# Linear attention and a gated feed-forward on one core: means of squares by transposes on VectorE, roots on GpSimd, weight scaling and copies of k^T v on ScalarE

## The chip, the cores and the metric

The kernel runs on one core of one Trainium2 chip. A core has TensorE (matrix products into PSUM), VectorE, ScalarE, GpSimd and a queue engine SyncE that issues most transfers. Each engine works off its own queue in order; semaphores tie the queues together. The time is that of one execution on the device in microseconds, and the median of several runs is compared. In the profile PE is TensorE, PEld its weight loads, DVE VectorE, ACT ScalarE, POOL GpSimd and SP SyncE.

## What is computed

```python
kv  = np.einsum('bhsd,bhse->bhde', k, v)            # 8 batches, 8 heads, 576 rows, 64 columns
o   = np.einsum('bhsd,bhde->bhse', q, kv)
rms = np.sqrt(np.mean(o * o, axis=-1, keepdims=True) + 1e-06)
a   = o / rms * g_norm                               # (8, 8, 576, 64)
x   = a.transpose(0, 2, 1, 3).reshape(4608, 512)
h   = x @ w_in                                       # 512 x 2048
sp  = np.maximum(h, 0) + np.log1p(np.exp(-np.abs(h)))
out = (h * erf(sp)) @ w_out                          # 2048 x 512
```

q, k, v and g_norm are float32. The two weight matrices come as 64-bit floats, which the kernel reads as pairs of 32-bit words.

## The kernel before

**Groups.** The 4608 rows are nine groups of 512: groups 0 to 7 are rows 0 to 511 of each batch, group 8 gathers the 64 rows that each batch leaves over. The attention of a group is worked out in four pairs of heads, called (T, p) with T the group and p the pair. Everything is kept transposed: 128 partitions hold the 2 x 64 columns of a pair, or 128 of the 2048 hidden columns.

**Four stages.** A list written out by hand (`ORDER`) computes the attention of group 0 and prepares the first weights. Then come 16 units of group 0 (n = 0 to 15), one for each 128 hidden columns: a hidden product in plain float32, its copy out of PSUM and the softplus on ScalarE, an Erf, the gate product on VectorE, and five units later (`LAG`) a projection. The attention of group 1 is worked out among them. Then 16 units of group 1 (n = 16 to 31), where the hidden product is made of three parts of lower precision (upper, lower and both), and where the weights are cut into such parts, written to memory and read again later. The attention of group 2 lies among these. The last four units of this stage have no projection between them; `held_sums` makes theirs at the end. From then on (about 240 us) 28 batches of four hidden products and four results follow; in the even ones the attention of the next group is made for two pairs of heads at once (`paired`).

**The order of a unit** (main loop from `for n in range(FIRST * FC + 1)`): perhaps `weights()`; `keep_prepared`; the pieces of place 3; the lower parts of cut weights; the pieces of place 0; `weights()` until what is due is joined; the gate product of unit n - 4 (group 0); the hidden product; its copy and softplus on ScalarE; the pieces of place 1; after every fourth unit of group 0 a batch of four Erf and the reload of the softplus table; the projection of unit n - 5; the pieces of place 2. The order on each engine is the order of the code.

**An attention in group 0's and group 1's units.** `visit` multiplies q by k^T v of its pair (two banks of PSUM, tile `at`), makes the products k^T v of the next pair in the same tile, and squares the result on ScalarE. One unit later `keep_tail` copies the left-over rows and `kv_kept` puts k^T v together: its halves lie in the wrong rows, so VectorE copies them across (line 371) and adds (line 372). `halve` splits the squares in an upper and a lower part, `mean` multiplies both by a matrix of 1/64 on TensorE (lines 470 and 471; for (1, 0) one product in plain float32, line 476), loads the table of logarithms on ScalarE, takes Ln, Exp and Square, and loads the softplus table again unless Erf follows. A unit later `norm` corrects the root by two operations on VectorE (lines 490 and 493), scales o (line 502) and `turn` transposes the next q (line 347). For (1, 0) the products k^T v come by themselves at unit 3 (`prepare`, line 395) and `keep_prepared` at unit 4 copies, adds and turns. The mean of the last pair, (2, 3), is left for `held_sums`.

**Weights.** `weights()` splits one weight tile, joins the one before and loads a later one. A split turns the 64-bit words into numbers: ScalarE scales the lower words (line 271). The upper words are scaled on ScalarE (line 270) during `ORDER`, and afterwards, with `w_late` set, on VectorE at the start of the join (line 281). The join goes on with a shift, an "and/or" and an addition of integers (lines 284, 287, 292).

**A pair of pairs, from 240 us.** `visit`, squares, `keep` (with `two_kept`: four copies on VectorE, line 380, and two adds) at place 2 of a batch; `block_sums` at place 3 (VectorE transposes the squares in blocks of 32x32 and sums 32 columns at a time); `across` at place 4 (four copies of 32x32 on ScalarE bring the sums of the other 32 rows beside them, VectorE adds); `root` at place 5 (Ln, Exp, Square between two table loads); `spread` at place 6 (two corrections, and a transpose of a broadcast that spreads the roots back); `norm` at place 8. Places 1 to 4 follow the four hidden products, 5 to 8 the four results.

**Buffers that matter.** The hidden products of group 1 use two banks by turns within a unit (one for `n_ps`, one for `m_ps`), so each unit needs the copies of the one before. From 240 us three pairs of banks go round. The tile `at` is one buffer.

Of the kernel before, what the change touches and what calls it, by code (L numbers as in the profile page):

```python
# [39 lines left out]
FP32 = mybir.dt.float32  # L40
# [8 lines left out]
EPS = 1e-6  # L49
# [10 lines left out]
BLOCKS = 16  # L60
ORDER = """
# [9 lines left out]
def kernel(  # L71
# [191 lines left out]
    def w_split(which, f, k):  # L263


        hi, lo, _ = words(which, f)
        e = early.tile([P, G * k], I32, name="w_e", tag="w_e", bufs=2)
        m = early.tile([P, G * k], I32, name="w_m", tag="w_m", bufs=2)
        if not w_late:
            nc.scalar.activation(e.bitcast(FP32), hi, AF.Copy, scale=2.0**-112)  # L270
        nc.scalar.activation(m, lo, AF.Copy, scale=2.0**-29)
        w_cv[which, f] = e, m, bool(w_late)

    def w_join(which, f, k):


        scaled, _, hi = words(which, f)
        e, m, late_ = w_cv.pop((which, f))
        w_raw.pop((which, f))
        if late_:  # L280
            nc.vector.tensor_scalar(
                out=e.bitcast(FP32), in0=scaled, scalar1=2.0**-112, scalar2=None, op0=ALU.mult
            )
# [17 lines left out]
    w_late = []  # L301
# [63 lines left out]
    def kv_kept(T, p, at, cols=kv_cols):  # L365
# [4 lines left out]
        for i in range(2):  # L370
            nc.vector.tensor_copy(out=other[rows_of[i]], in_=at[rows_of[1 - i], ::-1, cols])
        nc.vector.tensor_tensor(out=kv, in0=at[:, :, cols], in1=other, op=ALU.add)

    def two_kept(diagonal, beside):
# [3 lines left out]
        for i in range(2):  # L378
            for a, ps in enumerate((diagonal, beside)):
                nc.vector.tensor_copy(out=other[rows_of[i], :, a], in_=ps[rows_of[1 - i]])  # L380
# [22 lines left out]

    def attention(T, p):
# [3 lines left out]
        halves = T > 1 or (T == 1 and p > 0)  # L408
# [4 lines left out]
        two = halves_of  # L413

        bd = kv_of(T, p)

        def square_tile(name):
            return qt_tile(name)[:, 0:G]

        def visit():  # L420
# [24 lines left out]
            nc.scalar.activation(two(st["sq"]), st["o"], AF.Square)  # L445
# [9 lines left out]
        def halve():  # L455
            sq = st.pop("sq")
            hi = st["hi"] = attp.tile([P, G], FP32R, name="sq_hi", tag="rms_r")
            lo = st["lo"] = attp.tile([P, G], FP32R, name="sq_lo", tag="sq_lo")
            nc.vector.tensor_copy(out=hi, in_=sq)
            nc.vector.tensor_tensor(out=lo, in0=sq, in1=hi.bitcast(FP32), op=ALU.subtract)  # L460

        def mean(table=True):
            ms = st["ms"] = st["at"][:, :, 2 * P : 4 * P]
            parts = [(ms[:, a], a) for a in range(2)]
            if halves:


                hi, lo = two(st.pop("hi")), two(st.pop("lo"))
                for ps, a in parts:
                    nc.tensor.matmul(ps, lhsT=mean_w, rhs=hi[:, a], start=True, stop=False)  # L470
                    nc.tensor.matmul(ps, lhsT=mean_w, rhs=lo[:, a], start=False, stop=True)
                u = square_tile("u")
            else:
                u = st.pop("sq")
                for ps, a in parts:
                    nc.tensor.matmul(
                        ps, lhsT=mean_w.bitcast(FP32), rhs=two(u)[:, a], start=True, stop=True
                    )
            r = attp.tile([P, G], FP32, name="rms_r", tag="rms_r")
            exp_ln_table()  # L480
            st["u"], st["r"] = u, r
            nc.scalar.activation(two(r), ms, AF.Ln, bias=eps_col)
            nc.scalar.activation(r, r, AF.Exp, scale=-0.5)
            nc.scalar.activation(u, r, AF.Square)
            if table:
                softplus_table()

        def norm():
            ms, u, r = (st.pop(name) for name in ("ms", "u", "r"))
            nc.vector.scalar_tensor_tensor(  # L490
                out=two(u), in0=ms, scalar=EPS, in1=two(u), op0=ALU.add, op1=ALU.mult
            )
            nc.vector.scalar_tensor_tensor(
                out=u, in0=u, scalar=3.0, in1=r, op0=ALU.subtract, op1=ALU.mult
            )
# [4 lines left out]
            else:  # L500
                x = st["x"] = x_new.tile([P, G], FP32, name="x", tag="x")
            nc.vector.scalar_tensor_tensor(
                out=two(x),
                in0=st.pop("o"),
                scalar=gm_col,
                in1=two(u),
# [29 lines left out]
        pieces = (first_, (visit, loads), (halve, keep_tail) if halves else (keep_tail,))  # L536
        return (*(partial(chain, *group) for group in pieces), mean, partial(chain, norm, then_), split)
# [4 lines left out]
    def paired(T, p):  # L542
# [76 lines left out]
        def small(name):  # L619
            t = twice[name] = attp.tile([P, 2 * BLOCKS], FP32, name=name, tag=name)  # L620
            return t

        def block_sums():


            total = small("ms")
            for n in range(2):
                t = attp.tile([P, G], FP32, name="sq_t", tag=("rms_r", "sq_lo")[n])
                nc.vector.transpose(out=t, in_=twice["x"][n])
                nc.vector.tensor_reduce(  # L630
                    out=total[:, n * BLOCKS : n * BLOCKS + BLOCKS],
                    in_=t.rearrange("p (c d) -> p c d", c=BLOCKS),
                    axis=AX.X,
                    op=ALU.add,
                )

        def across():


# [812 lines left out]
```

## Time and profile before

| | us |
|---|---|
| median of 3 runs | 885.0 (884.7 to 885.28) |
| the profiled execution | 885.01, span 883.2 |
| a mean of squares: L470, L471 MATMUL 128x256, 14 each | 365 and 279 ns each |
| L281 VectorE scaling of upper words x13 | 677 ns |
| L270 ScalarE scaling of upper words, 128x1024 | 1157 ns |
| L371 VectorE copies of halves of k^T v x20 | 288 ns |
| L629, L630, L665 block transpose, sums, spread x24 each | 702, 686, 691 ns |
| L643 ScalarE copies 32x32 x48 | 215 ns |
| L482, L483, L484 Ln, Exp, Square 128x512 | 688, 631, 631 ns |
| table loads L114 x21 and L117 x43 | 1283 ns |

The mean length of a matrix product in the profile is longer than its distance to the next, since they are pipelined: the chain of waits, which counts from start to start, is the view that tells what one costs. The waits of TensorE that the profile puts on another engine are few:

| TensorE or its weight load waits for | us in total |
|---|---|
| VectorE's join of w_in (L292), before hidden products (L1201) | 3.0 |
| VectorE's xT of group 0 (L934) | 1.4 |
| VectorE's held gate parts (L719) | 1.0 |
| the transfer of w_out parts | 0.9 |

The largest waits of all are ScalarE's for TensorE's hidden products (91.8 us before the copy of line 1358) and for VectorE's sums (88.6 us before line 1363): idle time of an engine that isn't the bottleneck.

### The profile page before, as it was taken

What the parts mean: (1) busy time and instruction counts of PE and PEld (TensorE: products, weight loads), DVE (VectorE), ACT (ScalarE), POOL (GpSimd) and SP (SyncE); (2) the same over time, 40 slices, a digit from 0 to 9 for tenths busy, and PEclk for the clock granted to TensorE, in tenths of its full rate; (3) what the DMA queues carried; (4) which work ended last, traced back from release to release, by engine and by line L of the source; (5) the groups of instructions that cost most, each with busy time, mean ns of one, the idle gap of its engine ahead of it and who ended that gap; (6) DMA issues with size and microseconds to landing.
All of it is one profiled execution on the core that took longest, in us unless ns stands there. A gap on an engine that the chain in (4) does not pass through costs nothing.

```text
span 883.2 us, 13286 instructions
## 1 busy us (share of the span) xinstructions
PE 875.1 (99%) x4874; PEld 659.1 (75%) x4874; DVE 752.6 (85%) x1107; ACT 559.3 (63%) x789; POOL 4.7 (1%) x14
## 2 busy tenths in 40 slices
PE   8999999999999999999999999999999999999998
PEld 4444456666788888888888888888888888888887
DVE  5889978899998898989898989898979797966667
ACT  5977677777775657565665647474757575755552
POOL 2000000000000000000000000000000000000000
PEclk9999999999999999999999999999999999999999
DMA  9977427989799997999799979998797779778871
GB/s 291 291 225 224 132 75 285 342 310 341 262 358 401 330 347 251 385 328 349 232 382 350 353 231 346 366 342 295 272 351 282 288 288 344 289 279 334 316 255 49
DMA packets 136929, 259.89 MB, mean 294 GB/s; under 512 B 78816, under 2 KB 87264, under 8 KB 136864
## 3 DMA queue, kind: packets, MB, share of 16 engines
q1 hardware_dynamic: 136128, 258.09, 82.8%
q10 hardware_dynamic: 544, 0.82, 0.3%
q8 instruction: 39, 0.64, 0.3%
q14 instruction: 26, 0.21, 0.1%
q0 software_dynamic: 192, 0.13, 0.0%
HBM read 224.40 MB, written 34.60 MB: 293 GB/s over the span
## 4 chain that ended last, share of the span: by engine, by line
PE 91%; DMA 3%; DVE 2%; ACT 2%; issue 1%; SPq 0%; DVEq 0%; ACTq 0%
PE n_ps L778 48%; PE m_ps L778 24%; PE o_ps L834 8%; PE h_ps L1201 5%; DMA w_out_parts<-w_out 1%; PE at_ps L557 1%; DMA q_sb<-in_q_dram 1%; PE off_ps L588 1%; DMA w_in<-w_new 1%; PE warm_ps L982 1%; DMA w_in_parts<-w_in 0%; PE at_ps L427 0%; ACT s_sb L1154 0%; PE at_ps L440 0%; ACT L1154 0%
## 5 line engine op out<-in xcount | busy, mean ns | idle before, releaser
L778 PE MATMUL n_ps<-w_out_parts,g_forms 128*128 128x512 f32 (+1 forms) x936 | 230.1, 388 | 0.2 <-DMA w_out_parts<-w_out 0.2
L778 PE MATMUL n_ps<-x_forms,w_in_parts 128*128 128x512 f32 x896 | 222.6, 390 | 0.0
L778 PEld LDWEIGHTS n_ps<-w_out_parts,g_forms 128*128 128x128 f32 x936 | 175.0, 188 | 36.7 <-DMA w_out_parts<-w_out 0.9
L778 PEld LDWEIGHTS n_ps<-x_forms,w_in_parts 128*128 128x128 f32 x896 | 167.4, 188 | 35.1
L753 DVE TENSOR_TENSOR h<-m_ps,h 128x512 f32<-128x512 f32 x116 | 78.5, 686 | 58.6 <-PE m_ps L778 58.5
L1358 ACT ACTIVATE h<-n_ps 128x512 f32<-128x512 f32 x112 | 66.7, 596 | 94.0 <-PE n_ps L778 91.8
L1363 ACT ACTIVATE s<-h 128x512 f32<-128x512 f32 x112 | 69.2, 632 | 88.6 <-DVE h L753 88.6
L778 PE MATMUL m_ps<-w_out_parts,g_forms 128*128 128x512 f32 x464 | 123.9, 389 | 0.0
L778 PE MATMUL m_ps<-x_forms,w_in_parts 128*128 128x512 f32 x448 | 119.7, 389 | 0.0
L778 PEld LDWEIGHTS m_ps<-w_out_parts,g_forms 128*128 128x128 f32 x464 | 87.1, 188 | 18.1
L778 PEld LDWEIGHTS m_ps<-x_forms,w_in_parts 128*128 128x128 f32 x448 | 84.1, 188 | 17.5
L753 DVE TENSOR_TENSOR e<-m_ps,e 128x512 f32<-128x512 f32 x116 | 80.1, 692 | 14.1 <-PE m_ps L778 3.4
L834 PE MATMUL o_ps<-w_out_sb,h_sb 128*128 128x512 f32 x192 | 86.8, 595 | 0.0
L713 ACT ACTIVATE g_forms<-h 128x1024 fp32r<-128x1024 f32 x58 | 60.8, 1061 | 39.2 <-PE m_ps L778 21.0
L719 DVE SCALAR_TENSOR_TENSOR g_forms<-g_forms 128x1024 fp32r<-128x1024 f32 x58 | 71.1, 1226 | 2.0
L716 DVE TENSOR_TENSOR g_forms<-h,g_forms 128x1024 fp32r<-128x1024 f32 x58 | 70.5, 1215 | 0.5 <-ACT g_forms L713 0.4
L1412 DVE TENSOR_TENSOR h<-h,s 128x1024 f32<-128x1024 f32 x56 | 65.9, 1217 | 0.0
L834 PEld LDWEIGHTS o_ps<-w_out_sb,h_sb 128*128 128x128 f32 x192 | 35.5, 190 | 38.3 <-issue 36.9
L748 DVE SCALAR_TENSOR_TENSOR e<-n_ps,e 128x512 f32<-128x512 f32 (+1 forms) x89 | 59.8, 671 | 3.4 <-PE n_ps L778 3.4
L1201 PE MATMUL h_ps<-xT,w_in_sb 128*128 128x512 f32 x128 | 57.9, 596 | 1.3 <-DVE w_in_sb L292 1.2
L117 ACT ACT_TABLE_LOAD x43 | 55.2, 1283 | 0.8
L1386 ACT ACTIVATE s<-s 128x1024 f32<-128x1024 f32 x50 | 50.6, 1054 | 0.3
(166 smaller groups left out, 936.6 us busy)
## 6 DMA issues: line engine op xcount, KB each, us to landing
w_out_parts<-w_out SPq DMA_DIRECT2D x116, 768.0 KB, 7.2
w_in_parts<-w_in SPq DMA_DIRECT2D x112, 768.0 KB, 6.7
w_in<-w_new SPq DMA_DIRECT2D x16, 768.0 KB, 4.8
k_sb<-in_k_dram SPq DMA_DIRECT2D x32, 288.0 KB, 6.1
v_sb<-in_v_dram SPq DMA_DIRECT2D x31, 288.0 KB, 5.7
w_raw<-in_moe_w_in_dram SPq DMA_DIRECT2D x16, 512.0 KB, 6.3
w_raw<-in_moe_w_out_dram SPq DMA_DIRECT2D x8, 1024.0 KB, 5.3
out_dram<-e SPq DMA_DIRECT2D x32, 256.0 KB, 4.0
```

Source lines behind the costliest of these rows:

```text
L117: nc.scalar.preload_act_table_set("softplus")
L713: nc.scalar.activation(high, x, AF.Copy, scale=1.0 + 2.0**-13)
L716: nc.vector.tensor_tensor(out=low, in0=x, in1=high.bitcast(FP32), op=ALU.subtract)
L719: nc.vector.scalar_tensor_tensor(out=both, in0=low.bitcast(FP32), scalar=SHIFT, in1=high.bitcast(FP32), op0=ALU.mult, op1=ALU.add,)
L748: nc.vector.scalar_tensor_tensor(out=out_, in0=ps, scalar=scale, in1=out_, op0=ALU.mult, op1=ALU.add)
L753: nc.vector.tensor_tensor(out=out_, in0=ps, in1=out_, op=ALU.add)
L778: nc.tensor.matmul(ps[:, cols], lhsT=weights(form, k), rhs=moving(form, k)[:, cols], start=(form == forms[0] and k == 0), stop=(form == fo ...
L834: nc.tensor.matmul(o_ps[j], lhsT=g[:, j * P : j * P + P], rhs=one(w_out_sb, f), start=(f == 0), stop=last,)
L1201: nc.tensor.matmul(plain[i], lhsT=blocks_of(one(w_in_sb, i % FC))[:, c], rhs=xT[T][:, c, :], start=(c == 0), stop=(c == KC - 1),)
L1358: nc.scalar.activation(h[:, i], n_ps, AF.Copy, scale=SHIFT - 1.0)
L1363: nc.scalar.activation(s[:, i], h[:, i], AF.Softplus)
L1412: nc.vector.tensor_tensor(out=part(h, half), in0=part(h, half), in1=part(s, half), op=ALU.mult)
```

## The change

Every mean of squares is now made as the paired stage made its own: transposes and sums on VectorE, four copies across on ScalarE. The roots are no longer taken from ScalarE's tables but on GpSimd, by a first guess from the number's bits and three Newton steps: 15 operations on 128x16 (or 128x32) that follow one another. The spread by transposes replaces the corrections. ScalarE scales the upper words of all weights, and copies the halves of k^T v in `kv_kept` and `two_kept`. The mean of the last pair is no longer left for the end. The softplus table is loaded after every Erf batch of the paired stage. Gone are the products with the matrix of 1/64 among the units, and the table loads around the roots. The first attention (`ORDER`) is as before.

```diff
+NEWTON = 3
...
-        if not w_late:
-            nc.scalar.activation(e.bitcast(FP32), hi, AF.Copy, scale=2.0**-112)
+        nc.scalar.activation(e.bitcast(FP32), hi, AF.Copy, scale=2.0**-112)
         nc.scalar.activation(m, lo, AF.Copy, scale=2.0**-29)
...
-        if late_:
-            nc.vector.tensor_scalar(
-                out=e.bitcast(FP32), in0=scaled, scalar1=2.0**-112, scalar2=None, op0=ALU.mult
-            )
...
         for i in range(2):
-            nc.vector.tensor_copy(out=other[rows_of[i]], in_=at[rows_of[1 - i], ::-1, cols])
+            nc.scalar.copy(other[rows_of[i]], at[rows_of[1 - i], ::-1, cols])
         nc.vector.tensor_tensor(out=kv, in0=at[:, :, cols], in1=other, op=ALU.add)
...
-                nc.vector.tensor_copy(out=other[rows_of[i], :, a], in_=ps[rows_of[1 - i]])
+                nc.scalar.copy(other[rows_of[i], :, a], ps[rows_of[1 - i]])
...
+    def sums_of_blocks(squares):
+        total = small("ms", len(squares))
+        for n, x in enumerate(squares):
+            t = attp.tile([P, G], FP32, name="sq_t", tag=("rms_r", "sq_lo")[n])
+            nc.vector.transpose(out=t, in_=x)
+            nc.vector.tensor_reduce(
+                out=total[:, n * BLOCKS : n * BLOCKS + BLOCKS],
+                in_=t.rearrange("p (c d) -> p c d", c=BLOCKS),
+                axis=AX.X,
+                op=ALU.add,
+            )
+        return total
+
+    def roots(total):
+        n = total.shape[1] // BLOCKS
+        other, m, y, a = (small(name, n) for name in ("ms_other", "ms_eps", "rms", "rms_a"))
+        for k in range(4):
+            rows, beside = (slice(32 * i, 32 * i + 32) for i in (k, k ^ 1))
+            nc.scalar.copy(other[rows], total[beside])
+        two, one_ = nc.gpsimd.tensor_tensor, nc.gpsimd.tensor_scalar
+        two(out=m, in0=total, in1=other, op=ALU.add)
+        one_(out=m, in0=m, scalar1=EPS, scalar2=None, op0=ALU.add)
+        one_(
+            out=y.bitcast(I32),
+            in0=m.bitcast(I32),
+            scalar1=-0.5,
+            scalar2=float(0x5F3759DF),
+            op0=ALU.mult,
+            op1=ALU.add,
+        )
+        for _ in range(NEWTON):
+            two(out=a, in0=y, in1=y, op=ALU.mult)
+            two(out=a, in0=a, in1=m, op=ALU.mult)
+            one_(out=a, in0=a, scalar1=-0.5, scalar2=1.5, op0=ALU.mult, op1=ALU.add)
+            two(out=y, in0=y, in1=a, op=ALU.mult)
+        return y
+
+    def spread_over(xs, y):
+        for n, x in enumerate(xs):
+            nc.vector.transpose(
+                out=x.rearrange("p (c d) -> p c d", c=BLOCKS),
+                in_=y[:, n * BLOCKS : n * BLOCKS + BLOCKS].unsqueeze(2).to_broadcast([P, BLOCKS, 32]),
+            )
...
-            nc.scalar.activation(two(st["sq"]), st["o"], AF.Square)
+            nc.scalar.activation(halves_of(st["sq"]), st["o"], AF.Square, scale=0.125)
...
+        def block_sums():
+            st["ms"] = sums_of_blocks([st["sq"]])
+
+        def root():
+            st["r"] = roots(st["ms"])
...
-        pieces = (first_, (visit, loads), (halve, keep_tail) if halves else (keep_tail,))
-        return (*(partial(chain, *group) for group in pieces), mean, partial(chain, norm, then_), split)
+        pieces = (first_, (visit, loads), (keep_tail, block_sums), (root,), (norm, then_), (split,))
+        return (partial(chain, *group) for group in pieces)
...
-            pieces = first | {3: (block_sums,), 4: (across,), 5: (root,), 6: (spread,), 8: norms}
+            pieces = first | {3: (block_sums,), 4: (root,), 6: (spread,), 8: norms}
...
-    w_late.append(True)
...
-            steps[f + 2][3].append(halve)
-            with_erf = (f + 2) % BATCH == BATCH - 1
-
-            place = 2 if T < FIRST and p == 0 else 1
+            steps[f + 2][3].append(keep)
+            steps[f + 2][0].append(root)
             if T == FIRST and p == NP - 1:
-                ending.extend((partial(mean, table=False), norm, split))
+                ending.extend((norm, split))
                 continue
-            steps[f + 2][place].append(partial(mean, table=not with_erf))
...
-        mean, norm, split = ending
-        mean()
+        norm, split = ending
...
-            if not last_ and (b % 2 or not todo):
+            if not last_:
                 softplus_table()
```

In `norm` of both kinds the two corrections are replaced by `spread_over`, and o is scaled by `g_col` in place of `gm_col` (which held -0.5 times it).

## The prediction

> **What bounds the kernel now.** I read first the busy shares and the slices of the page.
>
> ```profile
> PE 875.1 (99%) x4874; PEld 659.1 (75%) x4874; DVE 752.6 (85%) x1107; ACT 559.3 (63%) x789; POOL 4.7 (1%) x14
> ...
> DVE  5889978899998898989898989898979797966667
> ```
>
> TensorE never rests for long, so the time is its work plus its few waits; VectorE is nearly full in the first 240 us (slices 2 to 11, of 22 us each), which is where most of the change lies. GpSimd does nothing after its start-up. Then the chain of waits in order of time. Between two products of group 0 stands one mean of squares:
>
> ```profile
> 66.16 3.43 PE h_ps L1201 x8
> 69.59 0.12 PE at_ps L470
> 69.71 0.12 PE at_ps L471
> 69.82 0.12 PE at_ps L470
> 69.94 0.12 PE at_ps L471
> 70.06 3.43 PE o_ps L834 x8
> ```
>
> The reader is to see that a mean costs the bounding engine 70.06 - 69.59 = 0.47 us, and that TensorE runs without a gap on both sides. From 50.78 to 195 us this chain is TensorE alone. Last I read the timeline of the engines at the places where the order of the queues changes (below).
>
> **What the change removes from TensorE.** Eight means: seven at 0.47 us are 3.3 us. The eighth, of (1, 0), is plain float32: TensorE ends a projection at 49.26 and starts the next hidden product at 50.78, 1.5 us with 0.5 us of waiting for weights. So at most 4.8 us, and nothing new is put on TensorE. Were this all, the time would be 885.0 - 4.8 = 880.2. That has to be set against who is now waited for.
>
> **Work that changes engine, by stage.** Group 0's units (22 to 129 us): VectorE loses 13 scalings (677 ns, 8.8 us); per attention it loses the halving (423 + 692), two root corrections (2 x 690) and two copies (2 x 288), and gains a transpose, a reduction and a spreading transpose (702 + 686 + 691): 1.0 us less each. ScalarE gains 13 scalings, 1.16 us by its one row of 128x1024, starting 1.05 apart, and per attention two copies 64x128 and four 32x32 (215 ns). The first are not shown on ScalarE; bounds are its 32x32 copy (215) and its 128x512 copy (586); I take 0.29, VectorE's own for that shape and on the line between the two by columns. ScalarE loses two table loads (1283 each) and three passes (688 + 631 + 631), 4.5 us each. In sums every engine but GpSimd gets lighter. All these hide behind TensorE if order lets them; order doesn't, at two places.
>
> **Place 1: the kv copies stand behind an Erf batch.** Unit 4 begins with `keep_prepared`: two copies of a half of k^T v, an add, and the transpose of q that the visit of (1, 0) multiplies. Unit 3 ended on ScalarE with a table load, four Erf and a table load.
>
> ```profile
> 36.86 0.59 ACT L1214 COPY h_sb<-h_ps 128x512 f32<-128x512 f32 x1 [0.57 <-PE h_ps L1201]
> 37.48 0.63 ACT L1230 ACTIVATE s_sb<-h_sb 128x512 f32<-128x512 f32 x1
> 38.12 1.28 ACT L1154 ACT_TABLE_LOAD   x1
> 39.42 2.19 ACT L1154 ACTIVATE s_sb<-s_sb 128x512 f32<-128x512 f32 x4
> 41.63 1.28 ACT L117 ACT_TABLE_LOAD   x1
> ...
> 37.67 0.59 DVE L371 COPY kv_other<-at_ps 64x128 f32<-64x128 f32 x2 [2.52 <-PE at_ps L395]
> 38.29 0.29 DVE L372 TENSOR_TENSOR bd_kv<-at_ps,kv_other 128x128 f32<-128x128 f32 x1
> 38.57 0.78 DVE L347 STREAM_TRANSPOSE qT<-q_sb 128x576 f32<-128x576 f32 x1
> ...
> 41.11 0.66 PE L427 MATMUL at_ps<-qT,bd_kv 64*64 64x256 f32 x8
> ```
>
> Now VectorE copies at 37.67 while ScalarE is busy, and q is ready at 39.35, before TensorE asks at 41.11. After the change the copies queue behind the Erf batch. ScalarE's new scaling in unit 2 (34.00) delays its chain by 1.05, of which 0.57 is eaten by the wait before 36.86: the last table load ends near 43.3. Two copies end at 43.85, the add at 44.2, the transpose at 45.0. TensorE's visit starts there: **3.9 us late**. Behind the waiting add on VectorE stand the join of w_out 0 (L284, L287, L292: 44.9 to 48.2), gate 0 (to 48.8), the tail copy and add (49.3), the new block sums (50.6) and the join of w_in 6 (3.2 us by its rows, to 53.8). TensorE, from 45.0: visit 1.17, hidden product 3.54, projection 3.43, is free at 53.15 and waits 0.65 for that join. The product that started at 50.78 starts at 53.8: **+3.0 us** with the first mean already taken off. The next units have room: the same ordering strikes at unit 8 (copies behind the Erf of unit 7, VectorE idle some 5 us), but gate 5, which I get at 85.9, is needed at 87.5.
>
> **Between.** Three means of group 0 and three of group 1 (0.47 each) take off 2.8: at unit 29 TensorE is +0.2. There keeps fall in units without Erf, and ScalarE's copies land where it idled (3.7 us before 140.94, 4.8 before 167.78).
>
> **Place 2: the last attention of group 1's stage (unit 30).** Here no projection separates hidden products 30 and 31, and both use the same two banks. On record now:
>
> ```profile
> 218.53 0.60 ACT L1216 ACTIVATE h<-n_ps 128x512 f32<-128x512 f32 x1 [0.37 <-PE n_ps L778]
> ...
> 219.25 0.42 PE L778 MATMUL n_ps<-x_high,w_new 128*128 128x512 f32 x1
> ```
>
> The bank is copied out by 219.13 and product 31 starts. After the change ScalarE's queue between Square (217.3) and that copy holds: two upper halves (to 218.3), four kv copies (to 219.35), then the four copies of `roots`, which wait for VectorE's block sums (adds at 219.7, sums to 221.0): to 221.95. Only then comes the bank's copy, to 222.55, so product 31 starts at 222.6 instead of 219.25. VectorE's `hold_lower` follows the late add (to 225.2 and 226.5), so the second held product starts at 226.55 instead of 224.23. The mean of 0.47 and two short waits that stood there are gone in this: **+2.3 us** from here on. Norm, split and the last gates move by the same 2.2 (the norm no longer waits 1.37 for ScalarE's roots, but VectorE comes later), so the transfers of w_out that start behind the last gates stay as hidden as now.
>
> **The paired stage (from 240 us).** Its TensorE work is the same, VectorE loses 0.55 us of small operations per pair, ScalarE a table load. Its copies of k^T v end when VectorE's did (Squares end 289.4, four copies to 290.4, adds to 291.0; now 291.2). New is that VectorE's spread (304.28 in the batch I followed) waits for 15 dependent GpSimd operations that can start when the 32x32 copies end (297.96). The nearest GpSimd rows are its memset of 128x256 (0.31) and
>
> ```profile
> 9.75 0.22 POOL L232 TENSOR_SCALAR gm_col<-g_col 128x1 f32<-128x1 f32 x1 [4.65 <-DMA g_col<-in_g_norm_dram]
> ```
>
> Between 0.22 and 0.31 us each, 15 make 3.3 to 4.7 us; 5.7 are there. I take 0.3. The next bank is needed at 308.46 and read out by 306.19, so the spread may be 2.3 us late before TensorE waits: GpSimd has 8.5 us in all, 0.57 per operation. Cost taken: nothing. The upper bound is that GpSimd and VectorE only take turns, which no row of this trace can exclude, as GpSimd is idle beside VectorE. In the pairs 2.8 us of VectorE's time before the spread reads one operand from PSUM; if only the two-operand rows (L719, L1412) shut GpSimd out, an operation may cost 0.42. In groups 0 and 1 VectorE has hardly other rows: some six GpSimd operations get in before the spread, the other nine cost 2.7 us and those six delay VectorE by 1.5, 4.2 us per attention. Gate 5 then comes at 90.1, 2.6 us too late for TensorE, and the held products 1 to 2 us later: +4 in sum, 891. A gain below nothing from GpSimd's part is excluded: no engine waits for less by it than is counted above.
>
> [...]
>
> **Sum.** 885.0 - 4.8 (means and the wait beside the first) + 3.9 + 0.65 (place 1) + 2.6 (place 2: 3.35 - 0.2 of late bank, less 0.55 of waits that go) = 887.35, that is 887.3 by the walk. The profiled execution took 885.01 (span 883.2 and 1.8 around it), the median is 885.0, so nothing is to be converted.
>
> **Rivals.**
> - *The gain survives* (881, 0.13): both delays are absorbed. For it: all engines get lighter in sums, and VectorE's 12 us of relief in group 0 might bring joins forward. Against: the visit depends on the late copies directly, and TensorE has no other wait after 50.78 to absorb 3 us. With one of the places absorbed: 884 to 885 (0.09).
> - *GpSimd shares VectorE's time* (891, range 889 to 896, 0.22): above; it decides as soon as spread waits show on VectorE over 3 us.
> - *GpSimd's chain outlasts the pairs' slack* (0.06): at 0.5 us an operation with VectorE shutting it out, the spread comes 3.4 us late, TensorE waits 1.1 us in each of 12 pairs: 887.3 + 4 + 13 = 904. It decides from 0.42 us per operation.
> - That the change doesn't do what it says I exclude: queue order is that of the code, and the rows of now follow it at every place read.
>
> **How the numbers follow.** The forecast (887.3, own range 885.5 to 889) has 0.50. A measurement of this kernel tells 0.2% (1.8 us) from no change: the border to slower is 886.8. Of the forecast 0.16 lies under it, and 0.09 for one place absorbed: same 0.25. Faster 0.13; slower 0.34 + 0.22 + 0.06 = 0.62. The range 883.0 to 893.5 leaves out most of the surviving gain below and the long GpSimd chain and the top of the shared case above.
>
> **What would show it.** Right: a TensorE wait of 3 to 4 us before L427 near 41 to 45 us, with kv copies on ScalarE behind the first Erf batch; a wait of about 3 us before hidden product 31; no means in the chain; steady pairs of 45.9 us for two batches as now. Wrong: the visit still near 41; VectorE waiting for GpSimd at the spreads; two batches longer than 45.9 (the chain's 335.29 to 381.22).

## The result and the profile after

| | before | after |
|---|---|---|
| median of the runs, us | 885.02 (884.7 to 885.28) | 896.21 (895.64 to 897.02) |
| profiled execution, its span, us | 885.01, 883.2 | 897.02, 895.2 |

The ratio is 1.0127 (95% interval 1.011 to 1.0145): slower by 11.2 us, where 2.3 were forecast and 893.5 was the upper end of the range. First the busy shares of the page after:

```profile
PE 879.0 (98%) x4842; PEld 658.7 (74%) x4842; DVE 720.9 (81%) x996; ACT 532.0 (59%) x804; POOL 131.7 (15%) x314
...
PEclk9989999999999999999999999999999999999999
```

TensorE has 32 instructions less and yet 3.9 us more of busy time; VectorE and ScalarE are lighter by 32 and 27 us. The clock that TensorE was granted (PEclk, in tenths of full speed) has a dent in the third of the 40 slices, 45 to 67 us. Next, from the list of waits by engine, TensorE's largest (in total, times, longest):

```profile
PE at_ps L469 <- DVE qT L342: 3.8, 1, 3.8
PE n_ps L746 <- ACT h L1179: 3.4, 1, 3.4
PE o_ps L802 <- DVE h_sb L1046: 2.1, 2, 1.5
```

The first is place 1, the second place 2, the third the gates of group 0. The timeline shows place 1 (start, length, engine, line, operation; in brackets the idle time before and who ended it):

```profile
44.12 0.29 DVE L367 TENSOR_TENSOR bd_kv<-at_ps,kv_other 128x128 f32<-128x128 f32 x1 [8.67 <-ACT kv_other L366]
44.40 0.78 DVE L342 STREAM_TRANSPOSE qT<-q_sb 128x576 f32<-128x576 f32 x1
45.33 1.13 PE L469 MATMUL at_ps<-qT,bd_kv 64*64 64x256 f32 x8 [3.82 <-DVE qT L342]
...
47.45 5.50 PE L1164 MATMUL h_ps<-xT,w_in_sb 128*128 128x512 f32 x8
```

VectorE stands 8.67 us for the copies that ScalarE makes behind its Erf batch, and the visit comes at 45.33 instead of 41.11. That was forecast. The last line was not: a hidden product that took 3.70 now takes 5.50. Place 2 is hidden product 31, whose bank is free only when ScalarE has copied product 30 out of it:

```profile
225.98 0.84 ACT L424 COPY ms_other<-ms 32x16 f32<-32x16 f32 x4 [1.75 <-DVE ms L409]
226.84 0.60 ACT L1179 ACTIVATE h<-n_ps 128x512 f32<-128x512 f32 x1
...
227.49 0.50 PE L746 MATMUL n_ps<-x_high,w_new 128*128 128x512 f32 x1 [3.39 <-ACT h L1179]
227.83 0.40 PE L746 MATMUL n_ps<-x_low,w_new 128*128 128x512 f32 x1
228.06 0.40 PE L746 MATMUL n_ps<-x_high,w_new 128*128 128x512 f32 x1
...
228.53 0.56 PE L746 MATMUL n_ps<-x_high,w_new 128*128 128x512 f32 x1
228.89 0.63 PE L746 MATMUL n_ps<-x_low,w_new 128*128 128x512 f32 x1
229.32 0.63 PE L746 MATMUL n_ps<-x_high,w_new 128*128 128x512 f32 x1
```

The bank's copy stands behind the four copies of `roots`, as forecast, and 1 us later the products go from 0.40 to 0.63 us each; from the start of one to the start of the next they go from 0.23 us (227.83 to 228.06) to 0.43 us (228.89 to 229.32). Compared at four marks (the first two by the chain of waits, the third by the timeline), the loss arises so:

| mark | before | after | late by | new here |
|---|---|---|---|---|
| hidden product 6 | 50.78 | 56.39 | 5.6 | 5.6 |
| first product of group 1 | 128.67 | 134.99 | 6.3 | 0.7 |
| first product of group 2 | 234.90 | 243.38 | 8.5 | 2.2 |
| end of the span | 883.2 | 895.2 | 12.0 | 3.5 |

### The profile page after: what moved, and what is told of

Same layout as the page of the kernel before. It is cut to its first block, busy times and chain, and to the rows that moved or that the text cites. A ratio compares the mean times of both kernels' runs of the same rounds, so it can differ in the third digit from the quotient of the medians.

```text
span 895.2 us, 13467 instructions
## 1 busy us (share of the span) xinstructions
PE 879.0 (98%) x4842; PEld 658.7 (74%) x4842; DVE 720.9 (81%) x996; ACT 532.0 (59%) x804; POOL 131.7 (15%) x314
## 4 chain that ended last, share of the span: by engine, by line
PE 88%; ACT 4%; DVE 3%; DMA 2%; POOL 2%; issue 1%; SPq 0%; DVEq 0%; ACTq 0%
PE n_ps L746 50%; PE m_ps L746 25%; PE o_ps L802 6%; PE h_ps L1164 1%; PE at_ps L567 1%; PE off_ps L598 1%; DMA v_sb<-in_v_dram 1%; DMA w_raw<-in_moe_w_in_dram 1%; PE n_ps L1062 1%; PE warm_ps L950 1%; ACT w_e L270 1%; ACT w_m L271 1%; PE at_ps L469 0%; ACT s_sb L1117 0%; PE at_ps L482 0%
## 5 line engine op out<-in xcount | busy, mean ns | idle before, releaser
L746 PE MATMUL n_ps<-x_forms,w_in_parts 128*128 128x512 f32 x896 | 224.9, 393 | 0.0
L426 POOL TENSOR_TENSOR ms_eps<-ms,ms_other 128x32 f32<-128x32 f32 (+1 forms) x20 | 15.2, 758 | 610.1 <-ACT ms_other L424 610.1
```

The costliest lines, as they stand in the source:

```text
L746: nc.tensor.matmul(ps[:, cols], lhsT=weights(form, k), rhs=moving(form, k)[:, cols], start=(form == forms[0] and k == 0), stop=(form == fo ...
```

## The experiments

Four theories were set against each other: **waits** (the two places), **clock** (TensorE is slower for a while after a rest), **GpSimd** (its chain costs VectorE time, by taking turns or by being waited for) and **layout** (the new small tile shifts all later ones). "Before" and "after" name the two kernels. All medians below stand against 884.9 to 885.1 for the kernel before on the same chip. In several expectations "3.70 us at 91.33" is called TensorE's wait for gate 5; that was a misread column: 3.70 is the length of the products there, the wait is 1.50 us.

### Layout

```diff
-        other, m, y, a = (small(name, n) for name in ("ms_other", "ms_eps", "rms", "rms_a"))
+        other, y, a = (small(name, n) for name in ("ms_other", "rms", "rms_a"))
+        m = other
```

> The sum with epsilon is written over ms_other instead of into a tile of its own, so that one small tile (128 bytes of each partition) is not allocated and all later tiles of that side lie where they lay in the kernel before; instructions and order are the same. Layout theory: the hidden products of the odd groups from 3 on take 2.72 instead of 2.79 us again, 12 batches of four of them, so 3.4 us less: 892.5 to 893.2. Rival (the odd groups' products are slowed by what GpSimd or ScalarE newly do beside them): 896 to 896.5, and 2.79 as before.

892.15 us (ratio to before 1.0078, 1.0061 to 1.0095), 4.1 less than after. And the other way round, in the kernel before:

```diff
-    const.tile([P, 8], FP32, name="pad")
+    const.tile([P, 40], FP32, name="pad")
```

> The kernel before, with an unused tile of constants longer by 128 bytes of each partition, so that all tiles of one side lie 128 bytes further on; not one instruction is different. Layout theory (the odd groups' hidden products depend on where their weights lie against x_forms): 12 batches of four products at 2.79 instead of 2.72 us, 888.0 to 888.6. Rival (the layout only mattered together with what the change does): 884.7 to 885.3.

889.06 us (1.0048, 1.0031 to 1.0064): 4.0 more, with no instruction changed. The groups of TensorE's rows from 240 to 880 us (count, busy time, mean ns of one), of before, after, the run with one tile less and before shifted:

```profile
L778 PE MATMUL n_ps<-x_forms,w_in_parts 128*128 128x512 f32 x880 | 218.7, 390 | 0.0
```

```profile
L746 PE MATMUL n_ps<-x_forms,w_in_parts 128*128 128x512 f32 x896 | 224.9, 393 | 0.0
```

```profile
L747 PE MATMUL n_ps<-x_forms,w_in_parts 128*128 128x512 f32 x896 | 222.7, 390 | 0.0
```

```profile
L778 PE MATMUL n_ps<-x_forms,w_in_parts 128*128 128x512 f32 x880 | 220.9, 393 | 0.0
```

The mean of 393 ns follows the 128 bytes and not the change. It hides two kinds, which the chain of after tells apart (start, length of eight products), an even and an odd group:

```profile
259.58 1.81 PE n_ps L746 x8
```

```profile
346.26 1.87 PE n_ps L746 x8
348.13 0.93 PE m_ps L746 x4
```

Only groups 3, 5 and 7 are slow: 2.79 instead of 2.72 us for a hidden product, 48 of them, 3.4 us. From the first product of group 2 to the end the kernels with the old addresses take 648.3 (before) and 647.7 (one tile less), those with shifted ones 651.8 (after) and 652.5 (before shifted). All 18 profiles fall into these two sets: 647.6 to 648.3 us in the eight kernels with the old addresses, 651.7 to 652.9 us in the ten with shifted ones, whatever else was changed. So the size of the loss at the fourth mark is shown, and its cause is where the tiles lie. Why these addresses are slower the runs do not tell.

### Place 1

```diff
-        kept.append(partial(kv_kept, T, p, at))
+        kept.append(partial(kv_kept, T, p, at, copy=nc.vector.tensor_copy))
```

> The two copies of k^T v that keep_prepared makes for the visit of (1, 0) go back to VectorE; all other copies stay on ScalarE. Waiting theory (the copies stand behind the first Erf batch, and the 4 us of rest cost TensorE's clock another 2 us): the visit starts near 41.2 instead of 45.33 us, hidden product 5 takes 3.54 instead of 5.43 us, and the first hidden product of group 1 comes at 129 to 130.5 instead of 134.99; 890.5 to 892 us in all. Rival (VectorE is short of time in group 0 anyway, so what is won there is lost again at gate 5, for which TensorE waits 3.70 us at 91.33): that wait grows to 6 us or more, and the time stays over 893.5.

895.39 us: 0.8 less than after. Neither theory had it: the time is over 893.5, as the rival said, but the wait for gate 5 did not grow to 6 us, it stayed at 1.48. The visit was on time, at 41.27; the chain tells what came instead:

```profile
43.41 1.14 ACT w_e L270
...
46.61 0.59 ACT qT L487
...
48.05 0.29 DVE bd_kv L367
48.34 0.63 DVE sq_t L408
...
49.59 0.69 DVE w_e L280
50.31 1.24 DVE w_e L283
51.57 1.24 DVE w_in_sb L288
...
52.95 5.37 PE h_ps L1164 x8
```

The new scaling on ScalarE makes the Square late (46.61, before 45.12), then come the copies on ScalarE and the block sums, and behind them the join that hidden product 6 needs, which before started at 46.79. So product 6 waits 3.37 us and again is slow. Two delays stood one behind the other, and taking away the first laid the second bare. To test this, the sums and the root of (1, 0) were put behind that join as well:

```diff
+        keep, root_ = [keep_tail, block_sums], [root]
+        if (T, p) == (1, 0):
+            root_.insert(0, keep.pop())
...
+            steps[f + 2][1 if (T, p) == (1, 0) else 0].append(root)
```

> The changed kernel with the copies for the visit of (1, 0) on VectorE, and with the block sums and the root of (1, 0) issued behind the join that hidden product 6 needs. Join theory (the first experiment won only 0.8 us because the join of w_in 6 then stood last, behind the scaling on ScalarE, the copies and the sums): visit at 41.3, join ended near 51.6, hidden product 6 at 51.6 instead of 52.95 after a wait of 2 us, and not slow; of the 3.4 us that this wins over the first experiment (1.4 of wait, 1.9 of clock) gate 5 may take up to 2 back: 892 to 894. Rival (VectorE's work up to gate 5 is the same, and all of it sets the end): 894.5 to 896.

893.32 us, as the join theory had it: product 6 at 51.33 after a wait of 2.2 us, at full speed (3.67 us), group 1 at 131.02.

### The clock

The first test put eight extra products ahead of the late visit, in a part of its own bank:

```diff
+            for _ in range(8 if (T, p) == (1, 0) else 0):
+                nc.tensor.matmul(prepared[0][:, 0, 0 : 2 * P], lhsT=xT[0][:, 0, 0:P], rhs=xT[0][:, 0, 0 : 2 * P], start=True, stop=True)
```

> The changed kernel with eight extra products in plain float32 (256 columns, into a part of the bank that nobody reads) ahead of the visit of (1, 0), so that TensorE works in the 3.8 us in which it waits for the late copies; the visit still waits. Clock theory (the rest itself makes TensorE slow for some 3 to 4 us afterwards): the visit stays at 45.3, its products and hidden product 5 run at full speed (1.2 and 3.5 us instead of 2.2 and 5.43), hidden product 6 starts at 54.4 when its join ends instead of 56.39. How much of the 2 us reaches the end depends on gate 5: if VectorE's work sets it, the wait at 91.33 grows and the time is 895.3 to 896.3; if not, 894 to 894.6. Rival (hidden product 5 is slow because something disturbs it, not because TensorE rested): 5.4 us as before.

899.17 us, and it did not test what it should: the extra products waited for the late add as well, so TensorE rested 2.97 us all the same, and they themselves took 5.38 us. The slow time fell on them, and hidden product 5 behind them took 3.70. With a free bank they needn't wait:

```diff
+                busy = ps_h.tile([P, G], FP32, name="busy_ps", tag="h")
+                for _ in range(8):
+                    nc.tensor.matmul(busy[:, 0 : 2 * P], lhsT=xT[0][:, 0, 0:P], rhs=xT[0][:, 0, 0 : 2 * P], start=True, stop=True)
```

> The test of the rest again, with the eight extra products in a bank that is free (their result isn't read), so that they needn't wait for the late add. Clock theory: they run from 41.3 to 45, the visit starts at 45.3 to 45.4 at full speed (1.2 us), hidden product 5 starts at 46.8 and takes 3.4 to 3.7 us instead of 5.43, hidden product 6 starts when its join ends, at 54.4, instead of 56.39; gate 5 then sets group 0, so the time is 895.2 to 896.4. Rival: 5.4 us for hidden product 5 as before.

895.37 us, within the clock theory's range. The same eight products took 3.62 us, and hidden product 5 behind the visit 3.70, not 5.50:

```profile
40.65 3.62 PE L469 MATMUL busy_ps<-xT 128*128 128x256 f32 x16
44.64 0.66 PE L479 MATMUL at_ps<-qT,bd_kv 64*64 64x256 f32 x8 [0.37 <-DVE qT L342]
...
45.82 3.70 PE L1174 MATMUL h_ps<-xT,w_in_sb 128*128 128x512 f32 x8
```

It is these lengths that decide; that the time lies in the range is in part luck. The expectation had gate 5 take the gain back. It took nothing: TensorE's wait for it is 1.48 us, as in after, and from the visit to group 1 it is 88.0 us (44.64 to 132.61) instead of 89.7 (45.33 to 134.99). But from group 2 on the profiled execution took 652.9 us instead of 651.8, for which the runs show no reason. The windows from 40 to 50 us (busy TensorE, weight loads, VectorE, ScalarE, GpSimd, then the granted clock, DMA share and GB/s), of after and of this run:

```profile
40.00:50.00 10.00, 6.18 (x55) 3.30 (x54) 5.21 (x9) 8.46 (x15) 0.00 (x0) 0.71 0.58 190
```

```profile
40.00:50.00 10.00, 9.63 (x76) 6.12 (x75) 5.85 (x10) 7.71 (x14) 0.00 (x0) 1.00 0.53 170
```

So this rest of 3.82 us cost twice, by its length and by the clock behind it: 0.71 against 1.00 in these windows. By single microseconds the clock of after is 0.64 in 44 to 45 us, 0.50 from 45 to 51, 0.95 in 51 to 52 and 1.00 from 52 to 55: some six microseconds at half, more than the 3 to 4 that the first expectation here took, an estimate of the author's. Place 2 shows that this has chance in it. The same wait of 3.4 us stands there in after and in this run:

```profile
226.00:230.00 4.00, 2.51 (x8) 2.04 (x9) 2.49 (x4) 3.06 (x8) 2.60 (x7) 0.83 1.08 372
230.00:234.00 4.00, 4.00 (x14) 3.16 (x14) 3.21 (x6) 1.67 (x3) 3.35 (x9) 0.75 0.86 227
```

```profile
224.00:228.00 4.00, 2.93 (x13) 2.40 (x14) 2.91 (x5) 3.14 (x7) 2.94 (x8) 1.00 1.06 355
```

From start to start the eight products behind that wait took 1.96 us here, 2.68 in after, 3.43 in the run with the join first and 3.58 in the run with only the norm later. What the clock cost in after is read against this run, where it stayed at 1.00: from the start of product 31 to the first held product 4.39 us (227.49 to 231.88) against 2.89, to group 2's first product 15.89 against 14.68. So the slow products took 1.5 us more, of which 1.2 reached group 2. The clock of after is 0.80 in 228 to 229 us, 0.50 from 229 to 232 and 0.99 in 232 to 233. Over all profiles the products behind waits of 1.45 to 2.2 us were at full speed (3.67 to 3.70 us for eight of group 0's 128x512, 0.66 for eight of a visit), and behind 18 of the 19 waits of 2.97 us or more they were not, at once or within about 1 us; the nineteenth is the 3.39 us of this run. The shortest with slow products behind them are 2.97 (the first test: 5.38 us for the extra products, which take 3.62 behind no rest) and 3.08 us (the run under "Scaling": 5.11 for eight). Why the same wait was followed by slow products in one run and not in another is not shown.

### Place 2

```diff
-            steps[f + 2][0].append(root)
+            steps[f + 2][1 if T == FIRST and p == NP - 1 else 0].append(root)
```

> The root of the last pair of group 1's units (the four 32x32 copies on ScalarE and the GpSimd chain) is issued one place later, behind the hidden product of unit 31 and its bank's copy; nothing else moves. Waiting theory: the wait of 3.39 us at 227.49 shrinks to about 0.7 (the four k^T v copies stay ahead of the bank's copy), the slow products behind it (2.88 and 1.71 us for halves that take 1.83 and 0.93) are fast again, and the time is 891.5 to 893.3. Rival (the late root only moves the wait to the norm and the held products of the last pair, which need the spread): TensorE waits as long some 10 us later, 895 to 896.5.

894.06 us, 2.2 less than after; 2.9 to 4.7 were expected. The wait is 0.79 instead of 3.39, the products behind it are at full speed (1.97 us from start to start for eight), and group 2 starts at 240.57, 2.8 earlier. Some 0.6 us come back as two waits of the held products for `hold_lower` (0.50 and 0.15). The rival, by which the wait only moves, is wrong by most of the amount.

### GpSimd and VectorE

Does GpSimd's work slow VectorE down? In the kernel before, 15 operations that nobody reads followed each of twelve gates:

```diff
             gates(done)
+            y = attp.tile([P, 2 * BLOCKS], FP32, name="rms_u", tag="rms_u")[:, 0:BLOCKS]
+            x = hs[done][:, 0:BLOCKS]
+            for _ in range(5):
+                nc.gpsimd.tensor_scalar(out=y, in0=x, scalar1=-0.5, scalar2=1.5, op0=ALU.mult, op1=ALU.add)
+                x = y
+                for _ in range(2):
+                    nc.gpsimd.tensor_tensor(out=y, in0=y, in1=y, op=ALU.add)
```

> The kernel before with a chain of 15 GpSimd operations on 128x16 after each of the gates 0 to 11 of group 0, whose result nobody reads: 180 operations in some 78 us, four times what the change puts there, and nothing waits for them. Turns theory (GpSimd and VectorE take turns, and both lose): VectorE's rows with two operands grow or start later, 0.2 us for most operations, some 20 us of VectorE in a stage where it is 94% busy: 890 to 905. Rival (only GpSimd loses: its operations stretch to 1.2 us, VectorE's rows stay, and the change lost time because VectorE waits in its queue for the end of the chain): 884.7 to 886.5, with GpSimd operations of 0.22 to 1.3 us.

885.55 us (1.0006, 0.9997 to 1.0016): no difference. The window of group 0, before and in this run:

```profile
50.00:128.00 78.00, 77.50 (x325) 35.95 (x324) 72.34 (x98) 55.63 (x72) 0.00 (x0) 1.00 0.58 174
```

```profile
50.00:128.00 78.00, 77.50 (x326) 36.14 (x325) 72.50 (x98) 54.88 (x71) 68.02 (x121) 1.00 0.55 174
```

GpSimd was busy for 68 of 78 us beside a VectorE that was busy for 72, and VectorE did its 98 instructions in the same time. Only GpSimd loses. How much is seen in the changed kernel's timeline, beside two-operand rows of VectorE and without them:

```profile
79.90 1.23 DVE L283 SCALAR_TENSOR_TENSOR w_e<-w_raw,w_e 128x1024 int32<-128x1024 int32 x1
80.02 1.19 POOL L438 TENSOR_TENSOR rms_a<-rms_a,ms_eps 128x16 f32<-128x16 f32 x1
...
81.27 1.23 DVE L288 CUSTOM_DVE_ANT_0 w_in_sb<-w_e,w_m 128x2048 uint16<-128x2048 uint16 x1
81.30 1.26 POOL L439 TENSOR_SCALAR rms_a<-rms_a 128x16 f32<-128x16 f32 x1
...
82.64 0.22 POOL L440 TENSOR_TENSOR rms<-rms,rms_a 128x16 f32<-128x16 f32 x1
82.94 0.22 POOL L437 TENSOR_TENSOR rms_a<-rms 128x16 f32<-128x16 f32 x1
...
85.29 0.71 DVE L447 STREAM_TRANSPOSE qT<-rms 128x512 f32<-128x512 f32 x1 [2.79 <-POOL rms L440]
```

While VectorE stands the operations of lines 438 and 439 take 0.22 and 0.20 us (83.24 and 83.55). Beside VectorE's long rows they took 1.19 and 1.26 and ended within 0.08 us of these: at 81.21 and 82.56, the rows at 81.13 and 82.50. Beside the shift of line 280, which has one operand (79.18, 0.69 us), one took 0.53. The chain takes 8.7 us, from 76.55 to 85.25, its second half undisturbed because VectorE stands and waits 2.79 us for it. Behind that wait in VectorE's queue are the spread, the norm, a turn, a join and gate 5 (90.59), for which TensorE waits 1.50 us. That VectorE is held up in its turn shows nowhere here: its 98 instructions took 72.50 us beside GpSimd's work and 72.34 without.

Would the chain be better on VectorE?

```diff
-        two, one_ = nc.gpsimd.tensor_tensor, nc.gpsimd.tensor_scalar
+        engine = nc.vector if n == 1 else nc.gpsimd
+        two, one_ = engine.tensor_tensor, engine.tensor_scalar
```

> The 15 root operations of the seven attentions in groups 0 and 1's units run on VectorE, 128x16 each; those of the pairs stay on GpSimd. Exclusion theory (GpSimd waits while VectorE reads two operands, and VectorE then waits for the chain: 14.5 us before its spreads of the units): VectorE's waits before these spreads go and 15 operations of some 0.07 to 0.15 us take their place, TensorE's wait of 3.70 us for gate 5 at 91.33 shrinks below 2, and the time is 893 to 895. Rival (gate 5 is late because VectorE started its joins late at place 1 and has too much to do): the wait stays 3 us or more, 895.8 to 897.

907.41 us, worse than either theory allowed: 15 operations cost VectorE 3.1 us (0.17 to 0.18 each and 0.21 from start to start, not 0.07 to 0.15, an estimate that no row shows: additions of 128x32 took 0.18 in the kernel before), and all stand ahead of a join. In the first of them the join of product 6 ended at 58.4 and group 1 started at 142.71; the wait at place 2 grew from 3.39 to 4.69.

With only the spread and the norm of the units moved behind the hidden product, and nothing else:

```diff
-            steps[f + 3][0].append(norm)
+            steps[f + 3][0].append(then_turn)
+            steps[f + 3][1].append(norm)
```

> The changed kernel with one thing moved: the spread and the norm of the units' attentions come behind the hidden product instead of ahead of joins and gates. Theory (gate 5 and the last gate of group 0 are late because VectorE stands in its queue and waits for the GpSimd chain): TensorE's waits of 1.5 and 0.56 us for these gates go, group 1 starts at 132.5 to 133 instead of 134.99; 893.7 to 894.5. Rival (VectorE's sum of work sets the gates): 895.5 to 897.

896.87 us, in the rival's range: the mechanism of the theory came, the gain didn't. Both gate waits are gone (one wait of 0.99 for the norm is left), and group 1 starts at 133.44, 1.55 earlier. But behind the wait at place 2, 3.39 us as ever, the clock fell for longer (0.81 from 220 to 228 us and 0.77 from 228 to 236; in after 0.83 from 226 to 230, 0.75 from 230 to 234 and 1.00 ahead and behind): group 2 starts at 242.90, only 0.5 earlier, and the stages from there take 652.4 instead of 651.8.

### Scaling

```diff
+        if not w_late:
+            nc.scalar.activation(e.bitcast(FP32), hi, AF.Copy, scale=2.0**-112)
...
+        if late_:
+            nc.vector.tensor_scalar(out=e.bitcast(FP32), in0=scaled, scalar1=2.0**-112, scalar2=None, op0=ALU.mult)
```

> The changed kernel with the upper words of the late weights scaled on VectorE again, as before; all else as changed. Waiting theory (the new scaling stands in front of the Erf batch and in front of the Square of (1, 0), 1.05 us each time): the visit of (1, 0) starts near 44.3 instead of 45.33, hidden product 6 near 55 instead of 56.39 as the 0.7 us more of the join give back part, gate 5's wait stays or grows, as VectorE has 13 scalings more; 894.5 to 896. Rival (VectorE's load in group 0 decides): 898 or more.

901.64 us, 5.4 more than after: the rival is right. Gate 5 is late by 3.08 us and the products behind it are slow (5.11 us). In the changed kernel VectorE's queue sets group 0, and this part of the change is a gain.

### What the means are worth

Means and roots alone: scaling and all copies of k^T v back on VectorE, one small tile less, the last root and the sums and root of (1, 0) later.

```diff
-            nc.scalar.copy(other[rows_of[i]], at[rows_of[1 - i], ::-1, cols])
+            nc.vector.tensor_copy(out=other[rows_of[i]], in_=at[rows_of[1 - i], ::-1, cols])
...
+            later = (T, p) in ((1, 0), (FIRST, NP - 1))
+            steps[f + 2][1 if later else 0].append(root)
```

> The means by transposes and the GpSimd roots alone: scaling and all copies of k^T v go back to VectorE, epsilon needs no tile of its own, the root of the last pair of group 1's units is issued behind unit 31's hidden product, and the block sums of (1, 0) and its root behind the join that hidden product 6 needs. Waiting theory: hidden product 6 starts at 50.8 as before the change, group 1 at 127.3 to 129.5 (three means of 0.47 less, gate 5 up to 2 us late because VectorE waits for GpSimd), no wait over 1 us at the last attention, 2.72 us products in odd groups; 881 to 884. Rival (GpSimd and VectorE shutting each other out costs most of the loss): gate 5 and later gates are 4 us or more late, 886 or more.

889.35 us, over the forecast and in the rival's range, though no gate is 4 us late: three are late by 1.55 to 2.24 us (5.6 in all), and VectorE stands 10.2 us before spreads of group 0's window. Then the norm later:

```diff
-            steps[f + 3][0].append(norm)
+            steps[f + 3][1].append(norm)
```

> As the run before (means and roots alone, placed later), and the spread with its norm and the turn of the next q is issued behind the hidden product instead of ahead of the unit's joins and gate, so that VectorE does not stand and wait for the GpSimd chain (2 us each time). Waiting theory: VectorE's waits before its spreads in the units fall from some 14 us to under 5, gate 5 no longer waits; 880 to 882. Rival (VectorE's waits were hidden anyway): the same time as the run before within 0.7 us.

885.93 us, 3.4 less but over the forecast. TensorE waits for no gate, but the turn of the next q went along and three visits wait for it (3.1 us). With the turn back where it was:

```diff
+            steps[f + 3][0].append(then_turn)
             steps[f + 3][1].append(norm)
```

> As the run with the norm later (means and roots alone), but the turn of the next q goes back ahead of the joins, where it waits for nothing; only the spread and the norm stay behind the hidden product. Queue theory (in group 0 what counts is how long VectorE stands still ahead of joins, gates and turns): the three waits of visits for the turn (1.5, 0.8, 0.8 us) go, group 1 starts at 127.5 to 128.7 instead of 130.77, 882.5 to 884. Rival (VectorE's sum of work sets group 0, and the waits only show where): gates or joins are late instead, 885 or more.

883.68 us (0.9985, 0.9975 to 0.9994), in its range; group 1 at 129.13, a little later than expected. With ScalarE scaling from the third late weight on:

```diff
-    w_late.append(True)
+    w_late.append(w_at["split"] + 2)
...
+            if what == "split" and w_late and i >= w_late[0]:
+                w_late.clear()
```

> As the run before in this call, and from the third late weight on ScalarE scales the upper words (the first two, which would stand ahead of the first Erf batch and of the Square of (1, 0), stay on VectorE). Queue theory: VectorE has 11 times 0.68 = 7.5 us less work, all behind hidden product 6, ScalarE has room there; no gate waits; group 1 at 127.2 to 127.8, 881.8 to 883. Rival (ScalarE's scaling delays copies and softplus, and so the gates): 884 or more.

882.71 us, in its range; group 1 at 128.15, 0.35 later than expected. The wait of 1.5 us before hidden product 6 was left; its join stood behind the copies and adds of (1, 0):

```diff
-            root_.insert(0, keep.pop())
+            root_[:0], keep[:] = keep, []
```

> The version that was below the kernel before (means and roots alone, turn first, norm later, late scaling on ScalarE from the third weight on), and at (1, 0) the whole of keep_tail, its sums and its root come behind the join that hidden product 6 needs. Theory (that join only waits for the Square through keep_tail): it ends before 49.3, hidden product 6 starts at 49.5 instead of 51.01, 881.0 to 881.5. Rival (the next thing in line, gates or the next visit, takes the 1.5 us back): 882.3 to 883.

881.14 us (0.9951, 0.9937 to 0.9965): faster than both kernels. Hidden product 6 starts at 49.88 without a wait. Its busy shares:

```profile
PE 871.2 (99%) x4842; PEld 655.8 (75%) x4842; DVE 736.9 (84%) x1054; ACT 517.2 (59%) x746; POOL 131.5 (15%) x314
```

TensorE is busy 3.9 us less than before the change, and the kernel is 4.0 us faster, near the 4.8 at most that were counted for the means. The order around them was changed as well, so the match is no proof that all of it is theirs.

## Why the prediction was wrong

**The gain of 4.8 us** was largely there to have: the last version is 4.0 us faster than the kernel before, with 3.9 us less work on TensorE. The change, 11.2 us slower, gave back more than three times the 4.8.

**Place 1** was right in its mechanism (visit 3.9 us late forecast, 4.2 measured, of which 0.3 stood already ahead of it: hidden product 4 started at 37.80 instead of 37.48 in the profiled execution) and mis-sized in its sum: +3.0 us at hidden product 6 forecast, +5.6 measured. The walk had TensorE work at full speed from 45.0; the visit's part took 2.20 instead of 1.17 and hidden product 5 1.9 us longer, 2.9 us of clock. The join that was to end at 53.8 ended at 54.36, but TensorE was late too and still had the projection to do, until 56.4, so the 0.65 us of waiting for the join fell away.

**Between**: "gate 5, which I get at 85.9, is needed at 87.5" failed. Gate 5 ended at 91.27, and two waits for gates (1.50 and 0.56 us) undid the three means of 1.4. The rival that named this, GpSimd sharing VectorE's time, had the place and the late gate right and the price wrong in kind: VectorE loses no busy time that the runs show (72.50 us against 72.34, above; the 1.5 us per attention of that rival no run shows), it stands in its queue, for 2.8 us at most where the rival's own sign was over 3. In the window from 50 to 128 us its busy time fell from 72.3 to 58.2 us, but it stood 8.4 us for roots and 6.3 for copies of k^T v, which before needed nobody.

**Place 2** was right to 0.05 us in its wait (3.35 forecast, 3.39 measured); the slow products behind it, 1.5 us of which 1.2 reached group 2, were missing.

**The paired stage** was costed at nothing. As to GpSimd that holds: VectorE's spreads wait 17.3 us for it there, in twelve waits of 1.4 at most, and yet with the old addresses the stage takes 647.7 us against 648.3 before the change. An operation took 0.40 us there on the mean (72.6 us for 180; the rival had 0.42): in the chain that starts at 305.85 us 0.22 to 0.29 beside rows of VectorE that read one operand from PSUM (lines 716 and 721), 1.17 and 1.10 beside those of line 1375, which read none. But the sum had no term for a new tile's 128 bytes, and these cost 3.5 of 12.0 us. No row of the profile before could show it; that the change allocates a tile stood in the diff.

So the step that failed is the sum: each wait was priced at its length, gate 5 was taken to be in time, and the paired stage was set at nothing. Clock (2.9 and 1.2 us, at the first and third mark), the waits for gates (2.1), layout (3.5) and the 0.3 ahead of place 1 make 10.0 us; less the 0.65 that fell away they are 9.4 of the 9.7 between the 2.3 forecast and the 12.0 by which the span grew. The other 0.3 stay open.

## What to carry to other kernels

In this kernel a wait of TensorE of 3 us or more had to be priced at its length and up to 2 to 3 us of slow products behind it; look at the granted clock behind such a wait. Small work moved to an idle engine was free here only for the busy engine's own time (VectorE's 72.50 us against 72.34): who waits for it in an in-order queue (VectorE, 2.79 us at most), and what stands behind that wait (gate 5, for which TensorE waits 1.50), was the price, and the remedy was to issue the waiting instruction later, with everything that does not need it ahead (889.35 us to 883.68). Where a change allocates or drops even a small tile, a run with the old addresses separates its layout from its work.

## What was not expected of the hardware

- A shift of all tiles of one side by 128 bytes of each partition made the eight-product runs of three groups take 1.87 instead of 1.81 us, 4 us in all, with the clock at 1.00.
- The same wait of 3.39 us left the next products between 1.96 and 3.58 us long in different executions.
- 121 operations of GpSimd in 78 us, beside a VectorE that is 93% busy, cost the kernel nothing that the runs can tell, while GpSimd's own operations took up to 1.26 us beside VectorE's two-operand rows (in the changed kernel) instead of 0.22.
